# Two places for K and V, one transfer per group of K, and a TensorE loop of two groups in a decode layer

## The chip, the cores and the metric

The kernel runs on one core of a Trainium2 chip. The metric is the device time of one execution in microseconds (us). Three executions of the kernel before took 195.89, 195.95 and 197.4 us; their median is 195.95. The profile is of one more execution, which took 195.84 us.

## The reference

One decode step of a parallel layer for four sequences: attention with a sliding window over a cache, and a gated MLP, both fed by the same normalised input and added to it. All tensors are bfloat16.

```python
B, Sq, D = 4, 1, 512
Hq, Hkv, Sk, Dh = 32, 8, 16384, 128
W = min(4096, max(256, Sk // 4))                 # the window: the last 4096 positions
xn = layernorm(x)
q = (xn @ wq) as (B, Hq, 1, Dh)
k = k_cache[:, :, Sk - W:, :]                    # each of the 8 heads serves 4 query heads
v = v_cache[:, :, Sk - W:, :]
p = softmax(q . k * Dh ** -0.5)
o = p . v
out = x + o.reshape(B, 1, Hq * Dh) @ wo + (silu(xn @ w_gate) * (xn @ w_up)) @ w_down   # F = 1792
```

The bulk of the data is the window of K and of V: 8 heads x 4 sequences x 4096 positions x 128 values x 2 bytes, 33.6 MB each. W_q and W_o are 4.19 MB each, W_gate, W_up and W_down 1.835 MB each.

## The kernel before, in words

A **group** is one of the eight key-value heads for all four sequences. On the 128 partitions lie 4 sequences x 32 blocks of positions; each partition holds NT = 128 positions of one sequence, so a group of K (or V) is a tile of 128 x 128 x 128 values, 4.19 MB, 32 KB in each partition.

**The head.** The vector engine normalises x; TensorE turns it (L377), projects it through W_q (L384) and through W_gate and W_up (L391). In all three the weights are the stationary operand and the four normalised rows the moving one. The scalar and vector engines make the gated product `guT`.

**The loop over the groups** on TensorE (L481) has, for one group r:

- `transposes` (L406): 16 chunks of 8 transposes, K tile by tile into PSUM (`ps_kt`, three banks); the vector engine (L322) or the scalar engine (L273) copies each chunk into `kT`;
- `scores` (L421), two chunks behind: K turned is the stationary operand, the 16 queries move;
- `fin` (L455, L457) of the group before, between chunks 2 and 3: sums its parts and its denominators;
- `maxima` (L428) and `shift` (L433): the vector engine has found the maxima (L328, L330, L333, L335, L337); a rank-limited matmul subtracts them and masks foreign sequences; the scalar engine takes the exponent into `p` (L276);
- `pv` (L442, L448): P times V, and the denominators;
- `spin` (L463): matmuls whose result nobody reads, 5 + 5 + 4 of them, in every group but the first (`eng.If(r > 0)`).

The groups' loops on the scalar and vector engines run over one group each and are not touched by the change.

**The order of the transfers** is written out by hand in `on_sync`; nearly all of them are issued by SyncE (SP) on one queue, and a wait in SP's program holds up all that stands behind it. There is one place for K (`KB`) and one for V (`VB`). The order is W_q (L249), W_gate, W_up, then for each group K in two halves (L239) and V (L244); W_down (L257) stands behind V of group 0, W_o (L247) in four pieces behind the last V. For every group but the first a half of K waits until TensorE has transposed the same half of the group before (`s_tr`, 16 per group), and V waits until `pv` of the group before is done (`s_pv`). TensorE in turn waits for a half of K ahead of chunks 0 and 8 (`d_k`), and for V ahead of `pv` (`d_v`).

**The tail.** After the loop come `fin`, `down` (L467 with W_down, added up in four strips of `acc4_ps`), the attention output put in order (L505, L366 into `oP`), and the products with W_o: rows 0 to 21, the first piece, go through `acc4` (L467), whose strips the scalar engine copies (L284) and a matmul with `sel4` adds to the last sum (L471); the other three pieces go through `acc` (L471). The result is copied (L369, L287) and stored by two small transfers.

Of the kernel before, what the change touches and what calls it, by code (L numbers as in the profile page):

```python
# [3 lines left out]
BF16 = mybir.dt.bfloat16  # L4
# [6 lines left out]
def bass_parallel_sum__sliding_block_cached__swiglu_ffn__decode_kernel(  # L11
# [12 lines left out]
    B, _, D = A_x.shape  # L24
    _, HKV, Sk, Dh = A_k_cache.shape
    HQ = A_wq.shape[1] // Dh
# [3 lines left out]
    NC = D // 128  # L30
# [6 lines left out]
    NT = W // NJ  # L37
    NH = B * REP
    CH = 8
    NCH = NT // CH  # L40
# [20 lines left out]
    KT = sb("kT", [128, 4, CH, 128], BF16, 512)  # L61
    P = sb("p", [128, NT, NH], BF16)
# [28 lines left out]
    ident = sb("ident", [128, 128], BF16)  # L91
# [17 lines left out]
    kt_ps = [t[:].bitcast(BF16).rearrange("p (a b) -> p a b", b=128) for t in ps_kt]  # L109
# [29 lines left out]
    s_const = sem("s_const")  # L139
    s_zero = sem("s_zero")  # L140
# [5 lines left out]
    s_q = sem("s_q")  # L146
# [3 lines left out]
    s_tr = sem("s_tr")  # L150
# [8 lines left out]
    s_pv = sem("s_pv")  # L159
# [12 lines left out]
    wq_ap = A_wq.rearrange("(p c) n -> p c n", c=NC)  # L172
    wg_ap = B_w_gate.rearrange("(p c) n -> p c n", c=NC)
    wu_ap = B_w_up.rearrange("(p c) n -> p c n", c=NC)
    wd_ap = B_w_down.rearrange("(p t) n -> p t n", t=NF)
    wo_ap = A_wo.rearrange("(p r) n -> p r n", r=NR)

    def kv_ap(cache, g, a, b):
        return cache[:, g, Sk - W:, :].rearrange("b (j t) d -> j b t d", j=NJ)[:, :, a:b, :]
# [51 lines left out]
        eng.drain().then_inc(s_zero, 1)  # L231

    def on_sync(eng):
        H = NT // 2

        def load_k(g, h):
            if g > 0:
                eng.wait_ge(s_tr, NCH * (g - 1) + (h + 1) * NCH // 2)
            eng.dma_start(KB[:, h * H:(h + 1) * H, :], kv_ap(A_k_cache, g, h * H, (h + 1) * H)).then_inc(d_k[h], 16)  # L239

        def load_v(g):
            if g > 0:
                eng.wait_ge(s_pv, g)
            eng.dma_start(VB[:], kv_ap(A_v_cache, g, 0, NT)).then_inc(d_v, 16)  # L244
# [4 lines left out]
        eng.dma_start(WQ[:], wq_ap).then_inc(d_wq, 16)  # L249
# [12 lines left out]
        eng.wait_ge(d_out, 32)  # L262
# [109 lines left out]
    def on_tensor(eng):  # L372
# [26 lines left out]
        eng.wait_ge(s_zero, 1)  # L399
        eng.wait_ge(s_guT, 1)  # L400

        def transposes(r, c):
            if c % (NCH // 2) == 0:
                eng.wait_ge(d_k[c // (NCH // 2)], r * 16 + 16)
            for k in range(CH):
                last = eng.transpose(kt_ps[c % 3][:, k, :], KB[:, CH * c + k, :], ident[:])  # L406
            last.then_inc(s_tr, 1)

        def scores(r, c):
            q = c * CH // BT  # L410
            if c % (NCH // NB) == 0:
                eng.wait_ge(s_p, r * NB + (q + 1))
                if q == 3:
                    eng.wait_ge(s_nrm, r + 1)
            if c in ACT_CH:
                eng.wait_ge(s_ea, r * len(ACT_CH) + (ACT_CH.index(c) + 1))
            else:
                eng.wait_ge(s_ev, r * (NCH - len(ACT_CH)) + (c + 1 - sum(a < c for a in ACT_CH)))
            for k in range(CH):
                t = CH * c + k - BT * q  # L420
                last = mm(ps_S[q][:, NH * t:NH * (t + 1)], KT[:, c % 4, k, :], QC[:],  # L421
                          start=(t == 0), stop=False, skip_group_check=True)
            if (c + 1) % (NCH // NB) == 0:
                last.then_inc(s_sc, 1)

        def maxima(r):
            eng.wait_ge(s_m, r + 1)
            eng.transpose(mT_ps, m16[:], ident[:]).then_inc(s_mt, 1)  # L428

        def shift(r):  # L430
# [6 lines left out]
        def pv(r):  # L437
            for t in range(0, NT, 2):
                n = t // 2 % 4
                if t % BT == 0:  # L440
                    eng.wait_ge(s_p, r * NB + (NB + t // BT + 1))
                mm(O_ps[32 * n:32 * n + 32, :], P[:, t:t + 2, :].rearrange("p t n -> p (t n)"),  # L442
                   VB[:, t:t + 2, :].rearrange("p t d -> p (t d)"),
                   start=(t < 8), stop=(t >= NT - 8), skip_group_check=True)
                if t % DT == DT - 2:
                    e = t // DT
                    n = e % 4
                    last = mm(den_ps[32 * n:32 * n + 32, :], ones[:, 0:32],  # L448
                              P[:, DT * e:DT * (e + 1), :].rearrange("p t n -> p (t n)"),
                              start=False, stop=(e >= NT // DT - 4), skip_group_check=True)  # L450
            last.then_inc(s_pv, 1)

        def fin(r):
            eng.wait_ge(s_dn, r + 1)
            mm(D2_ps, head[:], dsum[:], start=True, stop=True, skip_group_check=True)  # L455
            for h in range(2):
                last = mm(O2_ps, Osb[:, Dh * h:Dh * (h + 1)], sel[:, NH * h:NH * (h + 1)],  # L457
                          start=(h == 0), stop=(h == 1), skip_group_check=True)
            last.then_inc(s_fin, 1)

        def spin(n, k=2):
            for _ in range(n):
                mm(ps_kt[k][:], ones[:], own[:].unsqueeze(1).to_broadcast([128, 4, 128]),  # L463
                   skip_group_check=True)
# [13 lines left out]
            for t in range(NF):  # L478
                acc4(t % 4, guT[:, t, :], WD[:, t, :], t < 4, False)

        with eng.Fori(0, HKV) as r:  # L481
            for c in range(NCH):
                transposes(r, c)
                if c == 2:
                    fin(r)
                if c >= 2:
                    scores(r, c - 2)
            scores(r, NCH - 2)
            scores(r, NCH - 1)
# [12 lines left out]
        down()  # L502
# [1 line left out]
        for b in range(B):  # L504
            last = mm(perm_ps[:, NR * b:NR * (b + 1)], OT[:, b].rearrange("p k h q -> p (k h q)"), dr[:])  # L505
# [19 lines left out]


    on_sync(nc.sync)
    on_gpsimd(nc.gpsimd)
    on_scalar(nc.scalar)
# [29 lines left out]
```

## Time and profile before

| | |
|---|---|
| median of three executions | 195.95 us |
| profiled execution: time / span of the core | 195.84 us / 194.6 us |
| mean granted TensorE clock | 0.991 |
| bytes read from memory | 81.01 MB |
| busy: TensorE, vector, scalar, GpSimd | 162.3, 103.6, 61.6, 10.1 us |
| chain that ended last: transfers, TensorE | 66%, 28% |

The span runs from the first to the last instruction of the core; the execution's time has 1.24 us beside it. In rows of the timeline the first number is the start in us from the span's begin and the second the busy time. An L with a number is the line of the kernel; "PEld" is the loading of TensorE's stationary operand, "SPq" the queue of SyncE; `q1` is the queue of SP's transfers, `q8` and `q14` carry instructions. In a row of windows the stretch comes first, then its length, the busy time of each engine, the granted clock of TensorE, the busy share of the 16 DMA engines, and GB/s.

### The profile page before, as it was taken

How to read it: one execution, taken by the hardware profiler on the slowest of the kernel's cores; microseconds unless marked ns; L12 is line 12 of the kernel's file. 1: busy time of each engine (PE TensorE's matmuls, PEld its weight loads, DVE VectorE, ACT ScalarE, POOL GpSimd, SP SyncE). 2: the span in 40 equal slices, each digit the busy share in tenths (PEclk: the TensorE clock that was granted, in tenths of full speed). 3: DMA queues.
4: the chain of work that ended last, by engine and by line, in shares of the span. 5: the costliest groups of instructions: out<-in, count | busy, mean ns of one | idle time of the engine just before them, and what ended most of it. 6: DMA issues, size and time to landing. Idle time of an engine off the chain costs nothing.

```text
span 194.6 us, 7284 instructions
## 1 busy us (share of the span) xinstructions
PE 162.3 (83%) x3154; PEld 131.7 (68%) x3154; DVE 103.6 (53%) x218; ACT 61.6 (32%) x79; POOL 10.1 (5%) x49
## 2 busy tenths in 40 slices
PE   0009859995899989998999799979997999799994
PEld 0009859982798469845985698559855985698541
DVE  0071024683479347834783478347834783578341
ACT  1020001544054405440644064406440644064402
POOL 8750000000000000000000000000000000000000
PEclk9999999997899999999999999999999999999999
DMA  6999999999999899989999999999999999999992
GB/s 216 432 427 430 428 428 438 431 419 433 431 480 424 384 431 485 431 384 431 478 431 387 431 475 431 387 431 475 431 391 431 472 431 398 431 465 431 416 396 92
DMA packets 4639, 81.11 MB, mean 417 GB/s; under 512 B 524, under 2 KB 536, under 8 KB 920
## 3 DMA queue, kind: packets, MB, share of 16 engines
q1 hardware_dynamic: 4616, 81.01, 97.4%
q8 instruction: 5, 0.08, 0.1%
q14 instruction: 2, 0.02, 0.0%
q10 hardware_dynamic: 16, 0.01, 0.0%
HBM read 81.01 MB, written 0.00 MB: 416 GB/s over the span
## 4 chain that ended last, share of the span: by engine, by line
DMA 66%; PE 28%; DVE 2%; SPq 1%; issue 1%; ACT 0%; DVEq 0%
DMA kbuf<-in_A_k_cache_dram 43%; PE ps_kt L406 17%; DMA wo_sb<-in_A_wo_dram 12%; DMA wu_sb<-in_B_w_up_dram 11%; PE ps_s L421 4%; PE ps_s L457 2%; PE ps_o L391 2%; PE ps_kt L463 1%; PE ps_o L442 1%; SPq L247 1%; PE ps_s L455 1%; DVE kT L322 1%; PE ps_s L433 0%; DVE y_sb L369 0%; SPq L244 0%
## 5 line engine op out<-in xcount | busy, mean ns | idle before, releaser
L406 PE MATMUL ps_kt<-ident,kbuf 128*128 128x128 bf16 x1024 | 78.0, 223 | 8.6 <-DMA kbuf<-in_A_k_cache_dram 6.6
L322 DVE COPY kT<-ps_kt 128x1024 bf16<-128x1024 bf16 x88 | 57.6, 686 | 20.9 <-PE ps_kt L406 20.0
L406 PEld LDWEIGHTS ps_kt<-ident,kbuf 128*128 128x128 bf16 x1024 | 60.4, 99 | 11.9 <-DMA kbuf<-in_A_k_cache_dram 11.9
L273 ACT ACTIVATE kT<-ps_kt 128x1024 bf16<-128x1024 bf16 x40 | 40.9, 1023 | 66.2 <-PE ps_kt L406 66.2
L421 PE MATMUL ps_s<-qC,kT 128*128 128x16 bf16 x1024 | 44.8, 170 | 2.6 <-DVE kT L322 2.0
L421 PEld LDWEIGHTS ps_s<-qC,kT 128*128 128x128 bf16 x1024 | 37.9, 97 | 4.2 <-DVE kT L322 4.0
L276 ACT ACTIVATE p<-ps_s 128x512 bf16<-128x512 f32 x32 | 16.5, 603 | 34.1 <-PE ps_s L433 34.1
L328 DVE TENSOR_REDUCE mx<-ps_s 128x16 f32<-128x512 f32 x32 | 22.0, 689 | 6.2 <-PE ps_s L421 4.2
L463 PE MATMUL ps_kt<-own,ones 128*128 128x512 bf16 x100 | 25.3, 380 | 0.0
L442 PE MATMUL ps_o<-vbuf,p 128*32 128x256 bf16 x512 | 18.8, 286 | 0.3
L442 PEld LDWEIGHTS ps_o<-vbuf,p 128*32 128x32 bf16 x512 | 14.7, 100 | 6.1 <-ACT p L276 4.5
L340 DVE COPY osb<-ps_o 128x256 f32<-128x256 f32 x8 | 3.4, 424 | 28.6 <-PE ps_o L448 28.6
L448 PE MATMUL ps_o<-p,ones 128*32 128x256 bf16 x64 | 16.5, 284 | 0.0
L463 PEld LDWEIGHTS ps_kt<-own,ones 128*128 128x128 bf16 x100 | 8.0, 97 | 8.6 <-issue 1.5
L377 PE MATMUL ps_s<-i,xn 4*128 4x4 f32 x4 | 0.6, 254 | 14.4 <-DVE xn L308 14.4
L377 PEld LDWEIGHTS ps_s<-i,xn 4*128 4x128 f32 x4 | 0.6, 207 | 14.4 <-issue 14.4
L433 PE MATMUL ps_s<-cm,own 128*128 128x512 bf16 x32 | 8.7, 394 | 1.0 <-DVE cm L337 1.0
L448 PEld LDWEIGHTS ps_o<-p,ones 128*32 128x32 bf16 x64 | 6.5, 102 | 0.1
L433 PEld LDWEIGHTS ps_s<-cm,own 128*128 128x128 bf16 x32 | 2.5, 97 | 5.3 <-DVE cm L337 3.4
L294 DVE TENSOR_REDUCE st_sum<-x_sb 4x1 f32<-4x512 bf16 x1 | 0.7, 674 | 10.1 <-DMA x_sb<-in_A_x_dram 10.1
L457 PE MATMUL ps_s<-sel,osb 128*128 128x16 f32 x36 | 5.8, 275 | 0.0
L457 PEld LDWEIGHTS ps_s<-sel,osb 128*128 128x128 f32 x36 | 5.2, 208 | 0.0
(85 smaller groups left out, 76.0 us busy)
## 6 DMA issues: line engine op xcount, KB each, us to landing
kbuf<-in_A_k_cache_dram SPq DMA_DIRECT2D x16, 2048.0 KB, 13.9
vbuf<-in_A_v_cache_dram SPq DMA_DIRECT2D x8, 4096.0 KB, 16.4
wq_sb<-in_A_wq_dram SPq DMA_DIRECT2D x1, 4096.0 KB, 12.4
wo_sb<-in_A_wo_dram SPq DMA_DIRECT2D x1, 2816.0 KB, 22.5
wg_sb<-in_B_w_gate_dram SPq DMA_DIRECT2D x1, 1792.0 KB, 16.2
wu_sb<-in_B_w_up_dram SPq DMA_DIRECT2D x1, 1792.0 KB, 21.2
wd_sb<-in_B_w_down_dram SPq DMA_DIRECT2D x1, 1792.0 KB, 42.5
wo_sb<-in_A_wo_dram SPq DMA_DIRECT2D x1, 640.0 KB, 23.4
```

What stands on the lines that cost most here:

```text
L273: eng.activation(KT[:, c % 4], kt_ps[c % 3], ACT.Copy).then_inc(s_ea, 1)
L276: eng.activation(P[:, BT * q:BT * (q + 1), :], ps_S[q][:].rearrange("p (t n) -> p t n", n=NH), ACT.Exp, scale=SCALE).then_inc(s_p, 1)
L322: eng.tensor_copy(KT[:, c % 4], kt_ps[c % 3]).then_inc(s_ev, 1)
L328: eng.tensor_reduce(mx[:, q, :], ps_S[q][:].rearrange("p (t n) -> p n t", n=NH), AX.X, ALU.max)
L391: last = mm(o[:, t * B:(t + 1) * B], w[:].rearrange("p c (m t) -> p c t m", t=NF)[:, c, t, :], XnT[:, c, :], start=(w is WG and t == 0 and ...
L406: last = eng.transpose(kt_ps[c % 3][:, k, :], KB[:, CH * c + k, :], ident[:])
L421: last = mm(ps_S[q][:, NH * t:NH * (t + 1)], KT[:, c % 4, k, :], QC[:], start=(t == 0), stop=False, skip_group_check=True)
L433: mm(ps_S[q][:].rearrange("p (t n) -> p t n", n=NH), own[:], CM[:].unsqueeze(1).to_broadcast([128, BT, NH]), start=False, stop=True, skip_ ...
L442: mm(O_ps[32 * n:32 * n + 32, :], P[:, t:t + 2, :].rearrange("p t n -> p (t n)"), VB[:, t:t + 2, :].rearrange("p t d -> p (t d)"), start=( ...
L448: last = mm(den_ps[32 * n:32 * n + 32, :], ones[:, 0:32], P[:, DT * e:DT * (e + 1), :].rearrange("p t n -> p (t n)"), start=False, stop=(e ...
L457: last = mm(O2_ps, Osb[:, Dh * h:Dh * (h + 1)], sel[:, NH * h:NH * (h + 1)], start=(h == 0), stop=(h == 1), skip_group_check=True)
L463: mm(ps_kt[k][:], ones[:], own[:].unsqueeze(1).to_broadcast([128, 4, 128]), skip_group_check=True)
```

## The change

- `KB` and `VB` become two tiles each; group g uses number g modulo 2. W_q has no tile of its own any more: it lies in the second V tile, so that V of group 1 waits until the projection through it is done. W_o lies in the first K tile, so that it waits until the transposes of group 6 are done.
- K of a group comes by one transfer of 4.19 MB. From group 2 on K waits for the transposes, and V for `pv`, of the group two before.
- W_down is issued behind the last V, ahead of W_o.
- TensorE waits once per group for K. Its loop runs over four pairs of groups, with the code of both in its body; in the odd groups of a pair the filler matmuls need no `If`.

Nothing is changed in the head's matmuls: their weights are the stationary operand in both kernels.

```diff
-    KB = sb("kbuf", [128, NT, Dh], BF16, 512)
-    VB = sb("vbuf", [128, NT, Dh], BF16, 512)
-    WQ = sb("wq_sb", [128, NC, HQ * Dh], BF16, 512)
+    KB = [sb("kbuf%d" % u, [128, NT, Dh], BF16, 512) for u in range(2)]
+    VB0 = sb("vbuf0", [128, NT, Dh], BF16, 512)
+    VB1 = sb("vbuf1", [128, NT, Dh], BF16, 512)
+    VB = [VB0[:], VB1[:]]
+    WQ = VB1[:].rearrange("p t d -> p (t d)").rearrange("p (c n) -> p c n", c=NC)
...
-    WO = sb("wo_sb", [128, NR, D], BF16, 512)
+    WO = KB[0][:].rearrange("p t d -> p (t d)").rearrange("p (r n) -> p r n", r=NR)
...
-    d_v = sem("d_v")
+    d_v = [sem("d_v%d" % s) for s in range(2)]
...
     def on_sync(eng):
-        H = NT // 2
-
-        def load_k(g, h):
-            if g > 0:
-                eng.wait_ge(s_tr, NCH * (g - 1) + (h + 1) * NCH // 2)
-            eng.dma_start(KB[:, h * H:(h + 1) * H, :], kv_ap(A_k_cache, g, h * H, (h + 1) * H)).then_inc(d_k[h], 16)
-
-        def load_v(g):
-            if g > 0:
-                eng.wait_ge(s_pv, g)
-            eng.dma_start(VB[:], kv_ap(A_v_cache, g, 0, NT)).then_inc(d_v, 16)
+        def load(g):
+            u = g % 2
+            if g >= 2:
+                eng.wait_ge(s_tr, NCH * (g - 1))
+            eng.dma_start(KB[u][:], kv_ap(A_k_cache, g, 0, NT)).then_inc(d_k[u], 16)
+            if g == 1:
+                eng.wait_ge(s_q, 1)
+            if g >= 2:
+                eng.wait_ge(s_pv, g - 1)
+            eng.dma_start(VB[u], kv_ap(A_v_cache, g, 0, NT)).then_inc(d_v[u], 16)
...
         for g in range(HKV):
-            load_k(g, 0)
-            load_k(g, 1)
-            load_v(g)
-            if g == 0:
-                eng.dma_start(WD[:], wd_ap).then_inc(d_wd, 16)
+            load(g)
+        eng.dma_start(WD[:], wd_ap).then_inc(d_wd, 16)
+        eng.wait_ge(s_tr, NCH * (HKV - 1))
         for q in range(4):
             load_wo(q, WOS[q], WOS[q + 1])
...
-        def transposes(r, c):
-            if c % (NCH // 2) == 0:
-                eng.wait_ge(d_k[c // (NCH // 2)], r * 16 + 16)
+        def transposes(r, u, c):
+            if c == 0:
+                eng.wait_ge(d_k[u], (r - u) * 8 + 16)
...
-        with eng.Fori(0, HKV) as r:
-            for c in range(NCH):
-                transposes(r, c)
...
-            with eng.If(r > 0):
-                spin(5)
-            maxima(r)
-            with eng.If(r > 0):
-                spin(5)
-            shift(r)
-            eng.wait_ge(d_v, r * 16 + 16)
-            pv(r)
-            with eng.If(r > 0):
-                spin(4)
+        def warm(r, u, n):
+            if u:
+                spin(n)
+            else:
+                with eng.If(r > 0):
+                    spin(n)
+
+        with eng.Fori(0, HKV, 2) as r0:
+            for u in range(2):
+                r = r0 + u
+                for c in range(NCH):
+                    transposes(r, u, c)
...
+                warm(r, u, 5)
+                maxima(r)
+                warm(r, u, 5)
+                shift(r)
+                eng.wait_ge(d_v[u], (r - u) * 8 + 16)
+                pv(r, u)
+                warm(r, u, 4)
```

More of the change, by code (lines that the diff above doesn't have):

```diff
@@ L233, in on_sync @@
     def on_sync(eng):
-        H = NT // 2
-        def load_k(g, h):
-            if g > 0:
-                eng.wait_ge(s_tr, NCH * (g - 1) + (h + 1) * NCH // 2)
-            eng.dma_start(KB[:, h * H:(h + 1) * H, :], kv_ap(A_k_cache, g, h * H, (h + 1) * H)).then_inc(d_k[h], 16)
-        def load_v(g):
-            if g > 0:
-                eng.wait_ge(s_pv, g)
-            eng.dma_start(VB[:], kv_ap(A_v_cache, g, 0, NT)).then_inc(d_v, 16)
+        def load(g):
[8 more added lines that the diff above has]
+            eng.dma_start(VB[u], kv_ap(A_v_cache, g, 0, NT)).then_inc(d_v[u], 16)
         def load_wo(n, a, b):
             eng.dma_start(WO[:, a:b, :], wo_ap[:, a:b, :]).then_inc(d_wo[n], 16)
-        eng.dma_start(WQ[:], wq_ap).then_inc(d_wq, 16)
+        eng.dma_start(WQ, wq_ap).then_inc(d_wq, 16)
         eng.dma_start(WG[:], wg_ap).then_inc(d_wg, 16)
@@ L400, in on_tensor @@
         eng.wait_ge(s_guT, 1)
-        def transposes(r, c):
-            if c % (NCH // 2) == 0:
-                eng.wait_ge(d_k[c // (NCH // 2)], r * 16 + 16)
+        def transposes(r, u, c):
+            if c == 0:
+                eng.wait_ge(d_k[u], (r - u) * 8 + 16)
             for k in range(CH):
-                last = eng.transpose(kt_ps[c % 3][:, k, :], KB[:, CH * c + k, :], ident[:])
+                last = eng.transpose(kt_ps[c % 3][:, k, :], KB[u][:, CH * c + k, :], ident[:])
             last.then_inc(s_tr, 1)
@@ L435, in shift, with pv @@
                    start=False, stop=True, skip_group_check=True).then_inc(s_mk, 1)
-        def pv(r):
+        def pv(r, u):
             for t in range(0, NT, 2):
@@ L442, in pv @@
                 mm(O_ps[32 * n:32 * n + 32, :], P[:, t:t + 2, :].rearrange("p t n -> p (t n)"),
-                   VB[:, t:t + 2, :].rearrange("p t d -> p (t d)"),
+                   VB[u][:, t:t + 2, :].rearrange("p t d -> p (t d)"),
                    start=(t < 8), stop=(t >= NT - 8), skip_group_check=True)
@@ L479, in down @@
                 acc4(t % 4, guT[:, t, :], WD[:, t, :], t < 4, False)
-        with eng.Fori(0, HKV) as r:
-            for c in range(NCH):
-                transposes(r, c)
[L484 to L489, printed above, removed]
-            with eng.If(r > 0):
-                spin(5)
-            maxima(r)
-            with eng.If(r > 0):
-                spin(5)
-            shift(r)
-            eng.wait_ge(d_v, r * 16 + 16)
-            pv(r)
-            with eng.If(r > 0):
-                spin(4)
+        def warm(r, u, n):
[9 more added lines that the diff above has]
+                    transposes(r, u, c)
+                    if c == 2:
+                        fin(r)
+                    if c >= 2:
+                        scores(r, c - 2)
+                scores(r, NCH - 2)
+                scores(r, NCH - 1)
+                warm(r, u, 5)
[5 more added lines that the diff above has]
+                warm(r, u, 4)
         fin(HKV)
```

## The prediction

> **What bounds the kernel now.** I read the page from the top, then the queue's answer, the 2 us windows, the chain in order of time and the timeline. First the page: DMA share by slice, bytes per queue, shares of the chain.
>
> ```profile
> span 194.6 us, 7284 instructions
> PE 162.3 (83%) x3154; PEld 131.7 (68%) x3154; DVE 103.6 (53%) x218; ACT 61.6 (32%) x79; POOL 10.1 (5%) x49
> ...
> DMA  6999999999999899989999999999999999999992
> ...
> q1 hardware_dynamic: 4616, 81.01, 97.4%
> q8 instruction: 5, 0.08, 0.1%
> ...
> DMA 66%; PE 28%; DVE 2%; SPq 1%; issue 1%; ACT 0%; DVEq 0%
> ```
>
> The DMA engines are full in nearly every slice and lead the chain; TensorE is busy 83%, but part of that is filler (L463). The windows in mid-run and at the end give the rate:
>
> ```profile
> 86.00:88.00 2.00, 1.97 (x71) 1.75 (x72) 0.00 (x0) 1.54 (x4) 0.00 (x0) 1.00 1.01 434
> 88.00:90.00 2.00, 1.29 (x16) 0.35 (x6) 0.76 (x2) 0.00 (x0) 0.00 (x0) 1.00 1.02 434
> ...
> 188.00:190.00 2.00, 1.58 (x26) 0.73 (x30) 0.71 (x1) 0.00 (x0) 0.00 (x0) 1.00 0.92 374
> 190.00:192.00 2.00, 1.68 (x54) 0.64 (x42) 0.00 (x0) 0.60 (x1) 0.00 (x0) 1.00 0.42 164
> ```
>
> The last column is GB/s, the one before it the DMA share: full means 434 GB/s, and 81.01 MB at that rate are 186.7 us. Only the ramp ahead and the taper from 188 us on lie outside. The chain in order of time shows the beat of the groups:
>
> ```profile
> 28.52 2.74 PE ps_kt L406 x24
> ...
> 51.56 1.51 PE ps_kt L406 x24
> ...
> 148.49 1.51 PE ps_kt L406 x24
> ...
> 168.13 24.07 DMA wo_sb<-in_A_wo_dram
> 192.24 0.31 PE ps_s L471 x8
> 192.58 0.28 DVE y_sb L369
> ```
>
> Group 1 starts at 51.56, group 6 at 148.49: 19.39 us per group of 8.389 MB, that is 432.7 GB/s, the DMA rate. The end is W_o's last piece (168.13 + 24.07 = 192.20) and 2.4 us of small work. TensorE's reserve per group is read where group 6 ends and group 7 begins:
>
> ```profile
> 165.85 0.55 PEld L463 LDWEIGHTS ps_kt<-own,ones 128*128 128x128 bf16 x4 [0.21 <-issue]
> 165.85 1.04 PE L463 MATMUL ps_kt<-own,ones 128*128 128x512 bf16 x4
> 165.96 0.54 SPq L244 DMA_DIRECT2D vbuf<-in_A_v_cache_dram  x1
> ...
> 167.89 1.51 PE L406 MATMUL ps_kt<-ident,kbuf 128*128 128x128 bf16 x24 [1.00 <-DMA kbuf<-in_A_k_cache_dram]
> ```
>
> From 148.49 to 166.89 TensorE works (filler included); then it waits 1.00 us for the first half of K. So it is the slower partner by 1.0 us per group only: 18.4 against 19.4.
>
> **The change part by part.**
>
> *Two places for K and V.* SP's waits become looser by one group. What they gain depends on whether the queue ever ran dry. SP's issues and the time from issue to landing, of the window from 155 to 175 us:
>
> ```profile
> kbuf<-in_A_k_cache_dram SPq DMA_DIRECT2D x1, 2048.0 KB, 13.6
> vbuf<-in_A_v_cache_dram SPq DMA_DIRECT2D x1, 4096.0 KB, 16.4
> wo_sb<-in_A_wo_dram SPq DMA_DIRECT2D x1, 2816.0 KB, 22.5
> ```
>
> 2 MB take 4.85 us at the rate above but land 13.6 us after issue, 4 MB take 9.7 but land after 16.4: each transfer found about 7 to 9 us of other work queued ahead. The queue is never dry, so the second places make transfers be issued sooner, not move sooner. Gain 0; loss 0, since the new waits are long met: K of group g waits for the transposes of g-2, done about 11 us into a group, that is some 17 us before its own bytes could move; V waits for P·V of g-2, about 20 us ahead.
>
> *K in one transfer.* Eight transfers fewer. Bounds for one: nothing, and a third of what a group with its three transfers loses against the full rate: 8.389 MB at 434 GB/s are 19.33 us, measured 19.39, so 0.06/3 = 0.02 us. I take that end: 8 x 0.02 = -0.2 us at W_o's landing. The other side: transposes of a group now wait for all of K, 4.85 us later in the stream. The answer on waits shows eight waits of TensorE's weight loads for sixteen halves:
>
> ```profile
> PEld ps_kt L406 <- DMA kbuf<-in_A_k_cache_dram: 11.9, 8, 2.1
> ```
>
> one per group, so the second half was never waited for: the early half moves the group's start and nothing else.
>
> *W_down behind the last V.* Its 1.835 MB no longer stand ahead of K of group 1, so every K and V lands 1.835/0.4327 = 4.24 us earlier. With the whole K this nets out. K of group 7: the second half, issued last, starts its issue at 159.1 and lands 13.6 later:
>
> ```profile
> L239 SPq DMA_DIRECT2D kbuf<-in_A_k_cache_dram x16: 534/535/616, 2.2 to 159.1; - x16
> ```
>
> 159.1 + 13.6 = 172.7; less 4.24, less about 0.15 for the fewer transfers: 168.3, against 167.89 where group 7 starts now: TensorE's last group moves +0.4 us. W_down itself lands at about 182 us (9.84 us of W_o ahead of the end) and `down` starts at 186.95 (below): covered by 4 to 5 us; without that cover it would cost its remainder one to one. W_o waits for the transposes of group 6. The second half of K is issued when a group's transposes end, now at 159.1 for group 6, so at about 160, while V of group 7 and W_down (13.9 us) are still to move: never late. The same holds for W_q's place: V of group 1 waits for the projection through W_q, which TensorE has finished before its first transposes at 28.52, and its bytes can't move before about 52 us.
>
> *The tail.* What +0.4 us does there:
>
> ```profile
> 186.95 1.04 PE L467 MATMUL ps_s<-wd_sb,guT 128*32 128x512 bf16 x14
> ...
> 188.23 0.71 DVE L366 CAST oP<-ps_kt 128x128 bf16<-128x128 f32 x1 [0.36 <-PE ps_kt L505]
> ...
> 189.20 1.47 PE L467 MATMUL ps_s<-wo_sb,oP 128*32 128x512 bf16 x22 [0.42 <-DMA wo_sb<-in_A_wo_dram]
> ...
> 190.71 0.60 ACT L284 ACTIVATE s<-ps_s 128x512 f32<-128x512 f32 x1 [6.18 <-PE ps_s L467]
> 191.36 0.40 PE L471 MATMUL ps_s<-s,sel 128*4 128x128 f32 x8 [0.26 <-ACT s L284]
> 191.61 0.34 PE L471 MATMUL ps_s<-wo_sb,oP 128*4 128x128 bf16 x12
> 192.24 0.28 PE L471 MATMUL ps_s<-wo_sb,oP 128*4 128x128 bf16 x8 [0.29 <-DMA wo_sb<-in_A_wo_dram]
> ```
>
> oP is ready at 188.94 and W_o's big piece at 166.54 + 22.5 = 189.04: both end together now. With oP at 189.35 the 22 matmuls start about 0.3 later, the chain through L284 and L471 ends at 191.95 + 0.3 = 192.25 instead of 191.95, and the last eight matmuls start there instead of at 192.24 (W_o's last piece: 192.0). So W_o's wait is replaced by TensorE's own chain: net 0 to +0.1 us.
>
> *The start.* Group 0 now waits for the whole of K. V of group 0 landed at 3.49 + 38.9:
>
> ```profile
> 3.49 0.66 SPq L244 DMA_DIRECT2D vbuf<-in_A_v_cache_dram  x1
> ...
> DMA to landing us min/median/max: 15.1/16.4/38.9
> ...
> 50.92 0.54 SPq L244 DMA_DIRECT2D vbuf<-in_A_v_cache_dram  x1
> ```
>
> that is 42.4; K of group 0 is whole 9.7 us ahead, at 32.7, not 28.5; K of group 1 at 52.1, now without W_down between. Group 0 took 50.9 - 28.5 = 22.4 us (no filler, slow first transposes: 114 ns each in the first row of the chain, 63 later), so it ends at 55.1: TensorE is 3.0 us late for group 1. It wins back 1.0 per group: on time at group 4, nothing left at group 7. Price 0; bounds 0 and, were no reserve left, +3.0.
>
> *The unrolled loop.* Arithmetic and matmuls are the same; three of six branches around the filler go per two groups, 0.2 us of issue each, ahead of a wait for K: nothing. The new thing is code: the body has 353 matmuls with as many weight loads and about 75 other instructions, some 780, counted in the code; now twice that. All five instruction packets of q8 moved in the first pass:
>
> ```profile
> q8 instruction: 3, 0.05, 0.8%
> ...
> q8 instruction: 2, 0.03, 0.6%
> ```
>
> (windows 20:40 and 40:60; 3 + 2 are all five of the page, 16 KB each.) The six later back edges fetched nothing, so code of about 5 packets is held. The whole program grows from about 1,500 to 2,290 instructions: about 8 packets. No row shows whether these are held. Below: 0. Above: a fetch at each of three back edges. I take 0, since nothing came back at half the size, and price the rest as a rival.
>
> [...]
>
> **Sum.** Span 194.6 - 0.2 + 0.3 = 194.7 (transfers, then TensorE's chain taking over: nothing else on the path). The profiled execution took 195.84 us, 1.24 beside its span; the runs shown have a median of 195.95, 0.1 above it. 194.7 + 1.24 + 0.1 = **196.0 us**: no change. Its own range, from TensorE's group 7 starting with the DMA (-0.5) or 1 us later: 195.3 to 197.2.
>
> **The rivals.**
>
> *The doubled loop is fetched again (slower).* Place: TensorE's back edges after groups 1, 3 and 5. A fetch costs at least one packet's time (the window from 20 to 21 us: 5.9% of 16 engines for one us, 0.9 us), and at most what a small load takes behind a full queue:
>
> ```profile
> q8 instruction: 1, 0.02, 5.9%
> ...
> 3.34 0.63 ACTq L266 DMA_DIRECT2D x_sb<-in_A_x_dram  x1
> ...
> 10.13 0.67 DVE L294 TENSOR_REDUCE st_sum<-x_sb 4x1 f32<-4x512 bf16 x1 [10.13 <-DMA x_sb<-in_A_x_dram]
> ```
>
> 6.8 us. 1.0 us of it hides behind the four filler matmuls already queued. With 3 us, 2 remain: lateness 3.0, 4.0, 3.0, 4.0, 3.0, 4.0, 3.0 over groups 1 to 7, the end +3: **199 us**. With 0.9 us nothing; with 6.8 us 3.0 grows by 5.8 at three edges and falls by 1.0 per group, to 14.4: 210. It decides from about 2.7 us on. For it: the code doubles, the DMA engines are full. Against: not one packet after the first pass now.
>
> *TensorE becomes the bound (slower).* Group 0 on a cold array, whole K and 1.0 us of reserve: if the reserve is 0.4 and group 0 ends 4.5 us late, 2 us remain at group 7: **198 us**. Against: the 1.00 us wait above.
>
> *The deeper queue evens the sixteen engines (faster).* The taper holds (434-374)x2 + (434-164)x2 + 434x0.24 GB/s·us = 0.76 MB, 1.8 us. All of it gone: **194.2 us**. Against: the queue was deep enough at all times, the W_o pieces stay, and TensorE's chain ends with them.
>
> **How the numbers follow.** Forecast 0.70, fetch 0.19, TensorE 0.05, even engines 0.06. A measurement of this kernel tells about 1% (2 us) from no change. Beyond it: of the forecast 0.03 above, 0.02 below (one of the three runs shows 197.4); of the fetch 0.15 above; TensorE 0.05 above; even engines 0.04 below. Faster 0.06, same 0.71, slower 0.23. The range 195.0 to 199.5 leaves out the fetch beyond 3.2 us and the even engines, about 0.14.
>
> **What would show it.** Right: DMA share full from 6 to 188 us; K of group 7 whole and first transposes at 168 to 169; groups 5 to 7 each starting on a wait for kbuf; SP waiting only where the queue is deep; last W_o piece at about 192. A row of q8 with more than 9 packets and idle TensorE by "issue" after groups 1, 3, 5 would show the fetch. Group 7's transposes without a wait for K would show TensorE as the bound. Wrong altogether: a last W_o landing more than 2 us from 192.

## The result and the profile after

The changed kernel took **195.65 us** (median of 17 executions, 195.46 to 196.01); the kernel before, run beside it, took 196.01 (median of 17, 195.71 to 197.4). The ratio is 0.9976, with an interval from 0.9965 to 0.9987: a gain of 0.36 us, small but clear of no change. Of 50 executions of the kernel before that were taken beside the experiments, 16 show a mean granted clock below 0.977 and a median of 196.44, and 31 show 0.985 or more and a median of 195.89; none of the changed kernel's 17 lies below 0.98, so that against like executions the gain is 0.24 us. The profiled execution of the changed kernel took 196.01 us, the longest of its seventeen, so the end of its trace lies some 0.3 us late.

The page of the changed kernel, first its span, DMA share by slice and queues, then the shares of the chain:

```profile
span 194.8 us, 7252 instructions
...
DMA  6999999999999999999999999999999999999991
...
DMA packets 3490, 81.16 MB, mean 417 GB/s; under 512 B 396, under 2 KB 408, under 8 KB 792
q1 hardware_dynamic: 3464, 81.01, 97.0%
q8 instruction: 8, 0.13, 0.2%
...
PE 72%; DMA 16%; DVE 7%; issue 4%; SPq 1%; ACT 0%; DVEq 0%
```

The DMA engines are as full as before, yet the chain has turned over: TensorE 72% and DMA 16%, where it was 28% and 66%. q8 carried 8 packets instead of 5. q1 has 1,152 packets fewer: K of a group fills 128 partitions with one run each instead of two, which is 8 x 128 = 1,024, and the 128 others are small, 16 for each transfer saved.

The chain in order of time (start, duration, what):

```profile
32.78 2.74 PE ps_kt L407 x24
...
55.79 1.46 PE ps_kt L407 x24
...
61.24 0.81 issue
67.25 1.94 issue
...
69.98 2.15 PE ps_kt L464 x5
...
77.87 1.34 PE ps_kt L407 x24
...
96.09 1.34 PE ps_kt L407 x24
...
150.74 1.34 PE ps_kt L407 x24
...
168.96 1.34 PE ps_kt L407 x24
```

A row of `ps_kt L407 x24` opens a group. From group 2 on the groups start every 18.22 us ((168.96 - 77.87)/5), not every 19.4: TensorE runs at its own pace, not at the stream's. Group 1 took 22.08 us (55.79 to 77.87), with two stalls of 0.81 and 1.94 us in which it waited for nothing that the profile shows. The answers on waits and on q8 from 60 to 80 us, then the windows behind the stall:

```profile
PEld ps_kt L407 <- DMA kbuf<-in_A_k_cache_dram: 6.6, 1, 6.6
```

```profile
q8 instruction: 2, 0.03, 0.6%
```

```profile
68.00:70.00 2.00, 0.81 (x25) 0.75 (x26) 0.07 (x1) 0.00 (x0) 0.00 (x0) 0.86 1.06 459
70.00:72.00 2.00, 2.00 (x5) 0.45 (x3) 1.03 (x3) 0.00 (x0) 0.00 (x0) 0.50 0.99 426
```

TensorE waits for K once, at group 0, and never again. Code packets moved at 59 and at 66 us, each just ahead of a stall (61.24 and 67.25), and one more at 74, with no stall behind it. After the second stall the granted clock falls to 0.50 and the five filler matmuls (L464) take 2.15 us instead of 1.09 in the later groups. All packets but the last one, behind the loop (at 189), moved in the first pass (20 to 74 us): the back edges after groups 3 and 5 fetched nothing. The stream itself kept the beat that was foretold: SP's issue of K of group 7 and the time from issue to landing, then the same of W_o's last piece.

```profile
142.94 0.54 SPq L242 DMA_DIRECT2D kbuf<-in_A_k_cache_dram  x1
...
kbuf<-in_A_k_cache_dram SPq DMA_DIRECT2D x1, 4096.0 KB, 25.3
```

```profile
162.49 0.43 SPq L250 DMA_DIRECT2D kbuf<-in_A_wo_dram  x1
...
kbuf<-in_A_wo_dram SPq DMA_DIRECT2D x1, 256.0 KB, 29.5
```

K of group 7 landed at 168.24 (168.3 in the prediction) and TensorE came to it at 168.96, so it was still 0.72 us late; at group 2 it had been 6.35 late (77.87 against 47.42 + 24.1 = 71.52). W_o's last piece landed at 191.99, before at 168.13 + 24.07 = 192.20. The tail, from the timeline:

```profile
189.11 0.71 DVE L367 CAST oP<-ps_kt 128x128 bf16<-128x128 f32 x1 [0.36 <-PE ps_kt L513]
...
189.88 1.47 PE L468 MATMUL ps_s<-kbuf,oP 128*32 128x512 bf16 x22 [0.21 <-DVE oP L367]
...
192.26 0.46 PE L472 MATMUL ps_s<-kbuf,oP 128*4 128x128 bf16 x20
```

W_o's matmuls wait for DVE's copy (0.21), no longer for W_o's pieces.

### The profile page after: what moved, and what is told of

The parts are those of the page before. It is cut to its first block, busy times and chain, and to the rows that moved or that the text cites. A ratio compares the mean times of both kernels' runs of the same rounds, so it can differ in the third digit from the quotient of the medians.

```text
span 194.8 us, 7252 instructions
## 1 busy us (share of the span) xinstructions
PE 162.8 (84%) x3154; PEld 133.6 (69%) x3154; DVE 103.5 (53%) x218; ACT 61.6 (32%) x79; POOL 10.2 (5%) x49
## 4 chain that ended last, share of the span: by engine, by line
PE 72%; DMA 16%; DVE 7%; issue 4%; SPq 1%; ACT 0%; DVEq 0%
PE ps_kt L407 29%; DMA kbuf<-in_A_k_cache_dram 16%; PE ps_kt L464 12%; PE ps_s L422 11%; PE ps_o L443 9%; DVE kT L323 4%; PE ps_s L434 4%; PE ps_s L458 2%; PE ps_s L468 1%; PE ps_o L449 1%; PE ps_s L456 1%; PE ps_kt L429 1%; DVE mx L329 1%; DVE oP L367 0%; PE ps_s L472 0%
## 5 line engine op out<-in xcount | busy, mean ns | idle before, releaser
L407 PE MATMUL ps_kt<-ident,kbuf 128*128 128x128 bf16 x1024 | 78.4, 224 | 6.5 <-DMA kbuf<-in_A_k_cache_dram 6.5
L407 PEld LDWEIGHTS ps_kt<-ident,kbuf 128*128 128x128 bf16 x1024 | 61.2, 100 | 8.4 <-DMA kbuf<-in_A_k_cache_dram 6.6
L274 ACT ACTIVATE kT<-ps_kt 128x1024 bf16<-128x1024 bf16 x40 | 41.0, 1024 | 64.6 <-PE ps_kt L407 64.6
L464 PE MATMUL ps_kt<-own,ones 128*128 128x512 bf16 x100 | 26.6, 396 | 0.0
L449 PE MATMUL ps_o<-p,ones 128*32 128x256 bf16 x64 | 17.0, 289 | 0.0
L464 PEld LDWEIGHTS ps_kt<-own,ones 128*128 128x128 bf16 x100 | 8.2, 100 | 9.3 <-issue 2.7
## 6 DMA issues: line engine op xcount, KB each, us to landing
kbuf<-in_A_k_cache_dram SPq DMA_DIRECT2D x8, 4096.0 KB, 24.1
vbuf<-in_A_wq_dram SPq DMA_DIRECT2D x1, 4096.0 KB, 12.3
```

Of the source, the lines that this page charges most:

```text
L274: eng.activation(KT[:, c % 4], kt_ps[c % 3], ACT.Copy).then_inc(s_ea, 1)
L407: last = eng.transpose(kt_ps[c % 3][:, k, :], KB[u][:, CH * c + k, :], ident[:])
L449: last = mm(den_ps[32 * n:32 * n + 32, :], ones[:, 0:32], P[:, DT * e:DT * (e + 1), :].rearrange("p t n -> p (t n)"), start=False, stop=(e ...
```

## The experiments

Two questions stand open. What shortened the time by 0.36 us, when the DMA engines were full before and after? And did TensorE's lateness cost anything? The medians of the kernel before, beside these runs, are 195.90 to 196.08. The **warmed kernel** is that of the second experiment. Experiments are edits of the changed kernel where nothing else is said.

**K in two transfers again.** Everything else of the change stays.

```diff
-            eng.dma_start(KB[u][:], kv_ap(A_k_cache, g, 0, NT)).then_inc(d_k[u], 16)
+            for h in range(2):
+                eng.dma_start(KB[u][:, h * NT // 2:(h + 1) * NT // 2, :], kv_ap(A_k_cache, g, h * NT // 2, (h + 1) * NT // 2)).then_inc(d_k[u], 16)
-                eng.wait_ge(d_k[u], (r - u) * 8 + 16)
+                eng.wait_ge(d_k[u], (r - u) * 16 + 32)
```

> The changed kernel with K of each group in two transfers again; places, order and loop as changed. Theory A (eight transfers fewer brought the 0.36 us, as the term of the sum has it, 0.02 us each or a little more): W_o's last piece lands 0.2 to 0.4 us later than the 192.0 of the changed kernel, time 195.8 to 196.0. Theory B (the end of the changed kernel is TensorE's own chain, which never waits for K after group 0): no change, 195.65, and the groups start at the same times.

Measured: 195.91 us (195.83 to 196.28), ratio to before 0.9985 [0.9962, 1.0008]. That is theory A's figure: 0.26 us of the gain are gone, and the kernel is back at the 195.89 of the kernel before at like clock, so **the gain comes from K's transfer**; the places, the order and the loop together add nothing to it. The first transposes of group 7, in the chain, and the last matmuls, in the timeline:

```profile
140.87 27.55 DMA kbuf<-in_A_k_cache_dram
168.47 1.51 PE ps_kt L408 x24
```

```profile
191.95 0.59 PE L473 MATMUL ps_s<-kbuf,oP 128*4 128x128 bf16 x20
```

K of group 7 is late enough here for TensorE, otherwise unchanged, to wait for it. It landed at 140.87 + 27.55 = 168.42, that is 4.26 us ahead of the 172.7 of the kernel before, and W_down's move alone is worth 4.24. The last matmuls end at 192.54, before at 192.24 + 0.28 = 192.52.

**Filler from the start.** 18 filler matmuls ahead of the loop, and the filler in group 0 too, without a branch.

```diff
-            if u:
-                spin(n)
-            else:
-                with eng.If(r > 0):
-                    spin(n)
+            spin(n)
...
+        spin(18)
```

> The changed kernel with 18 filler matmuls while TensorE waits for K of group 0, and with the filler in group 0 too, so that no If is left. The first transposes should run at 58 to 63 ns instead of 114, group 0 end at about 52 instead of 55.8, and TensorE wait for K again from group 4 or so on. Theory B (TensorE's chain sets the end): 0.3 to 0.5 us faster than the changed kernel, 195.2 to 195.4, end then set by W_o's landing at 192.0. Theory C (the end of most runs is W_o's landing already, only the profiled run was later): no change, 195.6 to 195.7.

Measured: 195.54 us (195.36 to 195.69), ratio to before 0.9963 [0.9941, 0.9986]. This lies between the figures of the two theories. In the chain the first 24 transposes take 1.34 us behind the filler (56 ns each, at 34.66), where those of the changed kernel took 2.74 (114 ns, the prediction's "cold array") with the granted clock at 1.00 from 32 to 36 us, so that the clock does not show what slowed them. Group 1 starts at 53.34 instead of 55.79, and of its two stalls by "issue" one of 0.25 us is left. The timeline of this run:

```profile
110.03 1.51 PE L407 MATMUL ps_kt<-ident,kbuf 128*128 128x128 bf16 x24 [0.92 <-DMA kbuf<-in_A_k_cache_dram]
...
191.59 0.53 PE L472 MATMUL ps_s<-kbuf,oP 128*4 128x128 bf16 x20
```

and its chain:

```profile
139.97 28.09 DMA kbuf<-in_A_k_cache_dram
168.10 1.51 PE ps_kt L407 x24
```

Now TensorE waits for K in five groups (0.52 to 0.98 us each), and the stream's beat can be read: (168.10 - 110.03)/3 = 19.357 us. Before, K's first half came at 167.89 for group 7 and for group 3 at

```profile
90.26 1.51 PE L406 MATMUL ps_kt<-ident,kbuf 128*128 128x128 bf16 x24 [0.97 <-DMA kbuf<-in_A_k_cache_dram]
```

which is (167.89 - 90.26)/4 = 19.41. By these spans 0.05 us per group come from the whole K, 0.42 over eight. That is the upper end: K of group 7 landed at 139.97 + 28.09 = 168.06 here and at 168.24 in the changed kernel, against 168.42 with K halved, so 0.2 to 0.4 us by then, and the medians give 0.26 and 0.37 for the whole time. TensorE's lateness in the changed kernel cost some 0.1 us (195.65 against 195.54; the two were run at different times, and the kernel before moved by 0.07 between them). This is the fastest version of all, but only by that.

**W_down in its old place**, behind V of group 0, with the rest of the change.

```diff
+            if g == 0:
+                eng.dma_start(WD[:], wd_ap).then_inc(d_wd, 16)
-        eng.dma_start(WD[:], wd_ap).then_inc(d_wd, 16)
```

> The changed kernel with W_down behind V of group 0, as before. K and V from group 1 on land 4.24 us later: K of group 7 at 172.6 instead of 168.4, while TensorE would be free for it at about 169: it waits 3.6 us and everything behind it moves: span 198.4, time 199.2 to 199.6. If the place of W_down has no effect on the end (the transfers alone set it, all bytes being the same): 195.65.

Measured: 199.83 us (199.65 to 199.91), ratio 1.0179 [1.0123, 1.0234]. The chain:

```profile
172.39 1.51 PE ps_kt L408 x24
```

K of group 7 lands 4.29 us later than in the warmed kernel, against the 4.24 worked out in the prediction, and the time rises by 4.2, to a little above the range on record. The whole K pays only because W_down has left its way.

**W_down last in the kernel before.** One place for K and V, K by halves.

```diff
-            if g == 0:
-                eng.dma_start(WD[:], wd_ap).then_inc(d_wd, 16)
+        eng.dma_start(WD[:], wd_ap).then_inc(d_wd, 16)
```

> The kernel before with nothing but W_down moved behind the last V. Theory D (the gain is the tail's: K of group 7 earlier by 4.2 us, so oP is ready long before W_o's first piece): 0.2 to 0.4 us faster than before, 195.6 to 195.8. Theory A or C (the end is W_o's landing, same number of transfers and bytes): 196.0, last piece at 192.2 as before. A queue that runs dry because 4.2 us of cover are gone at the start (K of group 1 is issued 5 us, V of group 1 only about 1 us, before the queue ends): 0.5 to 2 us slower.

Measured: 199.2 us (198.53 to 200.07), ratio 1.0145 [1.0102, 1.0187]; more than was expected. Windows, then the timeline at the tail:

```profile
50.00:52.00 2.00, 1.97 (x60) 1.55 (x53) 0.40 (x2) 0.00 (x0) 0.00 (x0) 0.94 0.29 115
52.00:54.00 2.00, 2.00 (x39) 2.00 (x37) 2.00 (x5) 0.00 (x0) 0.00 (x0) 1.00 0.82 270
```

```profile
192.19 2.74 PE L466 MATMUL ps_s<-wo_sb,oP 128*32 128x512 bf16 x22 [4.69 <-DMA wo_sb<-in_A_wo_dram]
```

At 50 to 54 us the queue is dry (DMA shares of 0.29 and 0.82, where the kernel before has 0.99 and 1.02): (434 - 115) x 2 + (434 - 270) x 2 GB/s x us = 0.97 MB, 2.2 us of the stream. W_down behind V of group 0 was what had covered the single place there. At the tail TensorE idles 4.69 us for W_o and then runs its 22 matmuls in 2.74 us instead of 1.47. So the second places do pay, as cover for W_down's move, though they move no byte sooner by themselves (K of group 7 in the first experiment).

**The whole K in the kernel before**, with its one place: K waits for all transposes of the group ahead.

```diff
-                eng.wait_ge(s_tr, NCH * (g - 1) + (h + 1) * NCH // 2)
-            eng.dma_start(KB[:, h * H:(h + 1) * H, :], kv_ap(A_k_cache, g, h * H, (h + 1) * H)).then_inc(d_k[h], 16)
+                eng.wait_ge(s_tr, NCH * g)
+            eng.dma_start(KB[:], kv_ap(A_k_cache, g, 0, NT)).then_inc(d_k[0], 16)
```

(One transfer and one wait of TensorE per group; not shown.)

> The kernel before with one place and K of a group in one transfer, so that K waits for all transposes of the group before. The queue runs dry: V of a group moves for 9.7 us after its K, K of the next is issued at 10.6 us, takes about 2 us to start and 9.7 to land: 22.3 us per group instead of 19.4, about 20 us more in all: 213 to 220. If the queue still covered it: 196.

Measured: 246.09 us (one run). Windows:

```profile
96.00:98.00 2.00, 2.00 (x54) 2.00 (x50) 2.00 (x4) 1.29 (x2) 0.00 (x0) 1.00 0.00 0
...
114.00:116.00 2.00, 2.00 (x16) 2.00 (x15) 1.43 (x3) 0.00 (x0) 0.00 (x0) 0.50 0.91 393
```

In each group the queue is empty for some 6 us while TensorE works, then TensorE waits for K (4.6 to 5.4 us) and comes back at half clock (0.50 from 112 to 120 us), which delays its transposes and so the next issue: 24.4 to 27.1 us per group. The direction was expected, the half clock was not, and it explains most of what exceeds the figure on record: the next K is issued some 14 us into a group (99.76 - 85.62 = 14.14) instead of 10.6, and lands 12.5 us after its issue instead of 11.7 (9.7 of bytes, so 2.8 to start where the expectation has about 2; W_q, first in the queue, took 12.3). In the one group in which the clock was back after 3 us (from 139.12 on), the issue came at 11.88 us and the group took 24.35.

**The loop written out** for all eight groups: more code, no back edges.

```diff
-        with eng.Fori(0, HKV, 2) as r0:
+        for r0 in range(0, HKV, 2):
```

(Group 0 stays without filler, as in the changed kernel.)

> The changed kernel with TensorE's eight groups written out, no loop: every stretch of code runs for the first time. Theory F (the stalls by issue in group 1 of the changed kernel are code that arrives late through full DMA engines): such stalls in most of the groups 1 to 7, 0.3 to 2.7 us each as the profiles so far show, some 26 packets on q8 in all; TensorE's group goes from 18.2 to 19.5 on the mean, and the time to 196 to 200. Rival (only the first groups suffer, from something of the start): stalls in group 1 alone and 195.6.

Measured: 199.21 us (199.06 to 200.0), ratio 1.0166 [1.0128, 1.0203]. The page, then the timeline:

```profile
q8 instruction: 24, 0.39, 0.7%
```

```profile
171.11 1.51 PE L407 MATMUL ps_kt<-ident,kbuf 128*128 128x128 bf16 x24 [0.61 <-DMA kbuf<-in_A_k_cache_dram]
```

TensorE's own stalls are short (0.19 to 0.84 us, five of them, in groups 3 to 5) and it still waits for K of group 7: the delay is in the stream, where stalls in most groups had been expected. K of group 7 lands 3.0 us later than in the warmed kernel. By then 13 more packets of 16 KB had moved (20 against 7), 0.21 MB that at 434 GB/s would take 0.5 us; on the mean 0.23 us each. The delay comes in steps: by issue and landing 1.3 us at group 3, 1.6 at groups 4 and 5, 3.0 at groups 6 and 7.

**K and V in two transfers by partitions**, which keeps every run at 32 KB and should have told the number of transfers from the length of runs.

```diff
+            for h in range(2):
+                eng.dma_start(KB[u][64 * h:64 * h + 64], kv_ap(A_k_cache, g, 0, NT)[16 * h:16 * h + 16]).then_inc(d_k[u], 16)
```

(It replaces K's one transfer; V in the same way, and TensorE waits for both halves.)

> The changed kernel with K and V in two transfers each, cut by partitions: 64 partitions each, so the runs of 32 KB stay as they are and only the number of transfers grows, by 16. Theory A (a transfer costs the stream a fixed bit, 0.26 us for 8 of them where K was halved by positions): +0.4 to +0.6 us against the changed kernel, 196.1 to 196.3. Theory E (the 0.26 us came from the shorter runs, 16 KB instead of 32 KB): no change, 195.65.

Measured: 358.08 us, ratio 1.8243 [1.8182, 1.8303]. The page:

```profile
DMA packets 3746, 81.16 MB, mean 228 GB/s; under 512 B 652, under 2 KB 664, under 8 KB 1048
q1 hardware_dynamic: 3720, 81.01, 98.4%
```

The runs were as long as before, 256 small packets more, and the rate fell by almost half, with the queue never idle. The question was not answered: a transfer into 64 partitions is another thing than half a transfer into 128. It moved 228 GB/s where the changed kernel moved 417, and no run shows why.

**K and V in four transfers each by positions**: 48 transfers and 6,144 runs more.

```diff
+            for h in range(4):
+                eng.dma_start(KB[u][:, 32 * h:32 * h + 32, :], kv_ap(A_k_cache, g, 32 * h, 32 * h + 32)).then_inc(d_k[u], 16)
```

(It replaces K's one transfer; V in the same way, and TensorE waits for all four.)

> The changed kernel with K and V in four transfers each, cut by positions: 48 transfers more, runs of 8 KB. Theory A: 48 x 0.03 = 1.5 us more, 197.2 (196.9 to 197.6), W_o's last piece and K of group 7 later by as much. Theory E (short runs): more than that, since all runs are a quarter as long, but then without a loss where the cut is by partitions. Neither: 195.7.

Measured: 197.88 us (197.85 to 198.0), ratio 1.0091 [1.0057, 1.0124]. The timeline:

```profile
91.80 1.51 PE L409 MATMUL ps_kt<-ident,kbuf 128*128 128x128 bf16 x24 [1.04 <-DMA kbuf<-in_A_k_cache_dram]
...
150.68 1.51 PE L409 MATMUL ps_kt<-ident,kbuf 128*128 128x128 bf16 x24 [1.23 <-DMA kbuf<-in_A_k_cache_dram]
```

The beat is (150.68 - 91.80)/3 = 19.63, 0.27 more than with whole K and V. That is 0.045 us for each of 6 more transfers per group, or 0.35 ns for each of 768 more runs: the same line as the step from 19.357 to 19.41 by either count (0.05 per transfer, 0.41 ns per run). The whole time says the same: 2.34 us above the warmed kernel, 0.38 ns for each of 6,144 runs. That is more than the transfers' 0.03 us each on record allowed. The size is settled, the cause is not.

**Short runs in the same transfers.** The tiles of W_gate, W_up and W_down are padded, so that a partition's bytes no longer lie in one piece; this is an edit of the warmed kernel.

```diff
-    WG = sb("wg_sb", [128, NC, F], BF16, 512)
+    WG = sb("wg_sb", [128, NC, F + 64], BF16, 512)[:, :, 0:F]
-    WD = sb("wd_sb", [128, NF, D], BF16, 512)
+    WD = sb("wd_sb", [128, NF, D + 32], BF16, 512)[:, :, 0:D]
```

(W_up as W_gate.)

> The kernel of e2 (filler from the start) with gaps in the places of W_gate, W_up and W_down, so that the same three transfers write shorter runs: 3.5 KB instead of 14 KB, and 1 KB instead of 14 KB, 2,432 runs more, not one transfer more. Theory E (the price of K's halves and of the quarters, 2.2 us for 6,912 more packets, is that of shorter runs): 0.8 us more than e2, 196.2 to 196.5. Theory A (it is that of the transfers, 0.046 us each): as e2, 195.5.

Measured: 196.42 us (196.31 to 196.56), 0.88 above the warmed kernel. The page, then the timeline:

```profile
DMA packets 5922, 81.16 MB, mean 416 GB/s; under 512 B 396, under 2 KB 2200, under 8 KB 3608
```

```profile
110.42 1.51 PE L407 MATMUL ps_kt<-ident,kbuf 128*128 128x128 bf16 x24 [0.99 <-DMA kbuf<-in_A_k_cache_dram]
```

2,432 runs more, not one transfer and not one small packet more (396 as before). K of group 4 comes 0.39 us later (110.42 against 110.03), with 768 of these runs ahead of it (those of W_gate and W_up): 0.5 ns per run. Over groups 3 to 7 it is 0.33 to 0.43. The whole time gives 0.88/2,432 = 0.36 ns. SP's issue of W_o's first piece was held for 17.17 us here, but W_o's last piece still landed 14.3 us after its issue, so that the queue did not run dry there. **The number of runs makes the price**: 128 more runs in a group at 0.36 to 0.5 ns are 0.05 to 0.06 us, all that K's halves cost, and nothing is left for the number of transfers, which no run could change alone.

**Code on an idle engine.** The warmed kernel with 4,096 one-element memsets on GpSimd, written out, into a tile that nothing reads; GpSimd runs on to 550 us, so that only the stream up to the last group is of interest.

```diff
+        for n in range(4096):
+            eng.memset(pad1[32 * (n % 4):32 * (n % 4) + 1, n // 4:n // 4 + 1], 0.0)
```

> The kernel of e2 with 4,096 one-element memsets on GpSimd, which is idle after its start: nothing waits for them, and they add about 16 packets of code, as many as the written-out loop of e6 added. Theory G (in e6 K of group 7 landed 3.0 us later than in e2 because code packets hold up the DMA engines they use): K of group 7 and W_o land up to 3 us later, 197.5 to 198.7. Rival (e6's delay came from TensorE's own waits for code, which the stream then followed): as e2, 195.5 to 195.9.

Measured: q14 over the first 175 us, the timeline, and the windows at the end of the stream:

```profile
q14 instruction: 11, 0.09, 0.1%
```

```profile
173.11 1.51 PE L410 MATMUL ps_kt<-ident,kbuf 128*128 128x128 bf16 x24 [1.59 <-DMA kbuf<-in_A_k_cache_dram]
...
198.03 0.28 PE L475 MATMUL ps_s<-kbuf,oP 128*4 128x128 bf16 x8 [0.27 <-DMA kbuf<-in_A_wo_dram]
```

```profile
192.00:194.00 2.00, 2.00 (x27) 0.77 (x26) 1.21 (x4) 0.00 (x0) 1.43 (x16) 1.00 0.06 25
194.00:196.00 2.00, 1.59 (x36) 0.79 (x38) 0.16 (x1) 0.08 (x1) 1.44 (x16) 1.00 0.07 28
```

K of group 7 comes 5.0 us later than in the warmed kernel. At the end the stream runs at 25 to 28 GB/s with a share of 0.06 to 0.07, where the warmed kernel's stream is over by 192 (0.01). A rate of 25 to 28 GB/s is that of one engine in sixteen (434/16 = 27), so it seems that one engine had fallen behind and the end waited for it; the view does not tell the engines apart. The delay is larger than the 3 us on record.

**The same memsets in a loop** of 64 rounds: the writes stay, the code goes (one run).

```diff
+        with eng.Fori(0, 64) as i:
+            for n in range(64):
+                eng.memset(pad1[32 * (n % 4):32 * (n % 4) + 1, n // 4:n // 4 + 1], 0.0)
+            eng.drain()
```

> The kernel with 4,096 memsets on GpSimd again, but as 64 rounds of a loop over 64 of them, so that GpSimd's writes stay and its code does not have to be fetched (GpSimd itself runs on far beyond the result, so the time says nothing; the stream is read from the profile). If the code packets held up the stream: K of group 7 at 168.1 and W_o's last piece at 191.8 as in e2. If the memsets' writes did: 173 and 198, as with the straight code.

Measured, again q14 over the first 175 us and the timeline:

```profile
q14 instruction: 2, 0.02, 0.0%
```

```profile
168.20 1.51 PE L412 MATMUL ps_kt<-ident,kbuf 128*128 128x128 bf16 x24 [0.94 <-DMA kbuf<-in_A_k_cache_dram]
```

K of group 7 is back at its place. It was the code that held up the stream, not GpSimd's writes: 9 packets of 8 KB, 4.91 us, on the mean 0.54 us for each, where its bytes on one engine at 27 GB/s (the estimate 434/16) would take 0.30.

## Why the prediction was right and wrong

*Two places: gain 0.* Right in that no byte moves sooner for them: with K halved, K of group 7 came 4.26 us earlier, and W_down's move is 4.24 of it. But "nothing" hid their worth as cover: without them W_down at the end leaves the queue dry at 50 us (199.2), and the whole K does so in every group (246.09).

*K in one transfer: "8 x 0.02 = -0.2 us at W_o's landing."* Right in sign, and in the profiled run of the changed kernel in size (191.99 against 192.20); the medians say more, 0.26 us against the changed kernel and 0.37 against the warmed one, whose last piece landed at 160.64 + 31.1 = 191.74. So the term was mis-sized, and its cause misread. The prediction divided the stream's loss against 434 GB/s among three transfers and took the short count of transfers for the price. That rate was read in two windows of 2 us (the windows beside them show 393 and 426), and both lie where a half of K with its short runs was moving; 0.36 ns for each of a group's 384 runs would already be 0.14 us, where the prediction saw 0.06. The runs with padded weights and with quarters put the price on runs: 1,024 fewer at 0.36 ns are 0.37 us. With padded weights 768 more runs cost 0.39 us, at runs of 3.5 against 14 KB, in a stream that is full; shared evenly by the 16 engines that would be 48 runs and 8 ns each on an engine, an estimate.

*W_down behind the last V: 4.24 us earlier, netting out with the whole K.* Right: 4.29 measured, and K of group 7 landed at 168.24 in the changed kernel and at 168.06 in the warmed one, against 168.3 foretold.

*The tail: "+0.3".* **This is the step that failed.** The prediction let TensorE's own chain take over from W_o's landing and take back what the whole K gives, so that the sum came out at no change. From oP to the end of the last matmuls it reckoned 3.18 us: oP at 189.35, the chain's end at 192.25, then 0.28 for the last eight. Measured are 2.90 us in the changed kernel (189.11 + 0.71 = 189.82 to 192.26 + 0.46 = 192.72), 2.97 in the warmed one (188.44 + 0.71 = 189.15 to 191.59 + 0.53 = 192.12) and 3.02 with K halved (188.80 + 0.72 = 189.52 to 192.54). The 22 matmuls follow oP by 0.06 us, where the sum had 0.15; and the last twenty run in one piece of 0.46 to 0.59 us, where the sum had two of 0.34 and 0.28, as they stand around the wait for W_o's last piece in the kernel before. To this the sum added the upper end of its own "net 0 to +0.1". Without these the chain doesn't take back the stream's gain: the last matmuls end at 192.12 in the warmed kernel, 0.40 ahead of the 192.52 before. In the profiled run of the changed kernel they end at 192.72, but there TensorE began group 7 0.72 late.

*The start: "on time at group 4, nothing left at group 7", price 0.* Group 0 went as foretold (32.78, then 55.79 for 55.1). The reserve was right as well (19.36 - 18.22 = 1.1 us per group). What it left out is group 1: 2.75 us of stalls and a granted clock of 0.50 behind them, so that TensorE was 6.35 us late at group 2 and still 0.72 at group 7. That the price stayed at some 0.1 us is luck: eight groups were just enough.

*The unrolled loop: price 0, rival "fetched again".* The rival fell: no packet at the back edges. But the code did not come free. Its packets in the first pass coincide with the stalls of group 1, and the warmed kernel, in which filler covers the first pass, keeps only one of 0.25 us; that these packets caused them is argued from this, not isolated. The stream shows no price for the two further packets up to group 7: with K halved, K of group 7 came when the old time less W_down's 4.24 us has it (168.42 against 168.46). Why 13 packets of the written-out loop cost 3.0 us stays open.

*TensorE as the bound*, a rival at 198 us: its sign to look for came true, group 7's transposes started without a wait for K, but its price was almost nothing. *Even engines*, the rival at 194.2: not borne out; the last DMA slice is as thin as before.

"A measurement tells about 1% from no change" was too coarse: 17 executions of each told 0.2%. The sum mended: 194.6 - 0.26 (changed) or - 0.37 (warmed) for the whole K, 0 for the exchange of waits at the tail: 194.3 and 194.2 for the span; with the 1.24 and 0.1 of the prediction 195.7 and 195.6 for the time, measured 195.65 and 195.54.

## What to carry to other kernels

The stream of transfers is full nearly from end to end here, and each further run made it 0.36 to 0.5 ns longer: count the runs per partition, not only the transfers, and read the price from the beat of a landing over several groups (19.357 us with whole K and V, 19.63 with quarters). The second places moved nothing sooner, and yet with a single place the kernel with W_down last took 199.2 us and that with whole K 246.09: test the parts together and alone. Where one wait takes another's place at the end, add up the new chain from its operand on, without the pieces into which the old wait had cut it (0.46 us in one piece, where the kernel before had 0.34 and 0.28). Code that was read while the DMA engines were full was paid by the stream it goes through (4.91 us for 9 packets of GpSimd's); that TensorE paid for its own as well, by 2.75 us of stalls in group 1, is argued from their times alone.

## What the runs showed of the hardware beyond expectation

- One more run cost the full stream 0.36 to 0.5 ns (padded weights, runs of 1 and 3.5 KB instead of 14; quarters, 8 KB instead of 32: 0.38 ns). Times 16, for engines that share the runs evenly, that would be 6 to 8 ns on an engine, an estimate.
- Transfers into 64 partitions moved 228 GB/s with the queue at 98.4%, against 417 into 128.
- Code packets of GpSimd cost the full stream more than their bytes: on the mean 0.54 us for 8 KB (9 packets, 4.91 us), and the stream ended at 25 to 28 GB/s, a sixteenth of its rate. With 13 more packets of TensorE's, 16 KB each, it ran 3.0 us late, 0.23 us for each.
- After waits of 4.6 to 5.4 us for K the granted clock stood at 0.50 in the kernel before with whole K; the 22 matmuls of W_o took 2.74 us instead of 1.47 after a wait of 4.69, in that kernel with W_down last.
